# Decoding 64-bit MLP weights to float32: two ScalarE passes and one VectorE pass in place of one and three

## The chip, the cores and the metric

The kernel runs on one core of a Trainium2 chip. The metric is the device time of one launch in microseconds (us), the median of three runs. The core's engines are named as in the profile: PE is TensorE (PEld its weight loads), DVE is VectorE, ACT is ScalarE, POOL is GpSimd, SP is SyncE, which here only starts DMAs. Each engine executes its instructions strictly in the order of the program, and waits for others by semaphores.

## The reference

```python
scores = scale * q @ k.T - log(448)            # 4 batches x 12 heads, 448 x 448, head size 64
x = sigmoid(scores) @ v                        # -> (4, 448, 768)
h = relu(x @ w_in)                             # 768 -> 1024
u, v = h[..., :512], h[..., 512:]
v_n = (v - mean(v)) / sqrt(var(v) + 1e-6)
x = (u * (w_spatial @ v_n + b_spatial)) @ w_out    # 512 -> 768
xn = (x - mean(x)) / sqrt(var(x) + 1e-6) * g_ln
out = x + relu(xn @ w_ch1) @ w_ch2             # 768 -> 3072 -> 768
```

The weights w_in, w_out, w_ch1 and w_ch2 arrive as 64-bit floating-point numbers, which the kernel reads as pairs of 32-bit words, the low word first. It turns them into float32 on the chip. A 64-bit number has an 11-bit exponent and 52 bits of fraction: the high word holds the sign, the exponent and the upper 20 bits of the fraction, and float32 wants 3 more fraction bits, which are the top 3 of the low word.

## The kernel before

**Stages.** The attention runs first, heads in pairs, and hands its result batch by batch to the gated block (w_in, the spatial product, w_out). This stage lasts until about 370 us. Then comes the MLP with w_ch1 and w_ch2, in 24 steps of one weight group each: steps i = 0 to 11 (the loop at L1505) for eight row blocks of the output, the later ones over the same twelve groups for the other six. A group is 256 of the 3072 hidden columns and consists of four chunks of 128 x 768 weights (k = 0, 1 from w_ch1, k = 2, 3 from w_ch2).

**Products.** Nearly every float32 product is three matmuls of split operands (mm3, L317): both factors are split into a high part that PE takes at once (a cast on ACT) and the rest (a subtraction on DVE or POOL). The products with w_ch1 follow a scheme with seven block products in place of eight; B11, B21, T1, T2, B22, T3 and T4 are blocks of the weights or differences of such blocks, and A11, A12, S1, S2, S4, S3 and A22 the same of the activations. Two accumulators are involved in a step: X (a PSUM tile "ps1") and Y ("psa"). Y receives S1 x T1, is copied out by ACT (`copied`, L1258 to L1261, the copy at L1260), and then S4 x B22 is added to it in PSUM. So PE may begin S4 x B22 only after the copy. `summed` (L1263) adds such a copy to another accumulator on DVE (L1264), applies ReLU on ACT (L1266) and takes the low part on DVE (L1269). `ch2` multiplies the hidden block by w_ch2, eight row blocks one after another, and DVE adds each result to the output in SBUF (L911, the "chunk add").

**Decoding a chunk.** `w_scale` (L332 to L339) has ACT multiply the high word, read as a float, by 2^-112, which makes the exponent right and loses the low bits (L338, an ACTIVATE). `bit_ops` (L341 to L354) then makes three DVE passes: shift left by 3 (L345), OR in the low word shifted right by 29 (L347), OR in the sign of the high word (L351). In the attention stage, for groups 0, 1 and 3, `in_place` (L823) does the same inside the raw tile: the low word's shift (L827) and the scale (L828), then two DVE passes (L830, L833). Twelve chunks go this way; the other nine groups, 36 chunks, use `scale` and `bit` during the steps 0 to 11. The tile "q_all" or "m_all" holds raw words, "f_all" floats, "r_all" split parts.

**What sets the order.** The order is written out by hand. `plan1` (L1347) says for each spot of an MLP step which jobs are issued there: `s1` is `scale(1)`, `b1` is the next DVE pass of chunk 1, `T1` a split, `=T1` a difference, `w0` a split of a w_ch2 chunk. A `+` means the next group. In a usual step, spot A1 (right after X has been copied the first time) holds `+b0 +b0 +s1`, so the scale of chunk 1 stands on ACT ahead of the ReLU of `summed` and of the copy of Y. The third `b` of a chunk also issues the load of a later chunk into the raw tile (`load(k + 2)`, or for k = 2, 3 the next group's chunk). In the attention stage a stream (L998) takes jobs such as `i0` from a list, at a rate by assumed costs, and puts them between the attention's own instructions. `i0 i1` ahead of each other make a burst of two scale passes on ACT.

Of the kernel before, what the change touches and what calls it, by code (L numbers as in the profile page):

```python
# [9 lines left out]

F32 = mybir.dt.float32
F32R = mybir.dt.float32r
U32 = mybir.dt.uint32
AF = mybir.ActivationFunctionType
ALU = mybir.AluOpType

P = 128
# [20 lines left out]
WC = 768  # L38
# [116 lines left out]
class Block:  # L155
# [13 lines left out]
    def ap(self, *dims):  # L169
        a = self.bits(*dims)  # L170
        return a.bitcast(F32) if self.t.dtype == U32 else a

# [12 lines left out]
class Ring:  # L185
# [4 lines left out]
    def next(self):  # L190
        self.i += 1
        return self.blocks[(self.i - 1) % len(self.blocks)]
# [66 lines left out]
def sigmoid_attention_gmlp_mlp(ctx: ExitStack, tc, q, k, v, w_in, w_sp, w_out, g_ln, w1, w2, out):  # L259
    nc = tc.nc  # L260
    const = ctx.enter_context(tc.tile_pool(name="const", bufs=1))
# [5 lines left out]

    R = Arena("r", const.tile([P, R_SIZE], F32R, name="r_all"))
    plain = ctx.enter_context(tc.tile_pool(name="plain", bufs=1, side="right"))
    F = Arena("f", plain.tile([P, F_SIZE], U32, name="f_all"))  # L270
    raws = tc.tile_pool(name="raws", bufs=1, side="right")
    Q = Arena("q", raws.__enter__().tile([P, Q_SIZE], U32, name="q_all"))
    mid = tc.tile_pool(name="mid", bufs=1)
    M = Arena("m", mid.__enter__().tile([P, T_SIZE], U32, name="m_all"))
    vscr = dram.tile([NT, DH], F32, name="vscr")
# [18 lines left out]
    vstat = const.tile([P, B, 4, 2], F32, name="vstat")  # L294
    nc.vector.memset(vstat, 1.0)
    vnorm = const.tile([P, 2, B, 4], F32, name="vnorm")
    mhalf = const.tile([P, 2, 4], F32, name="mhalf")
    nc.vector.memset(mhalf, -0.5)

# [27 lines left out]
    def w_load(src, blk=None):  # L327
        raw = (blk or raw_r.next()).bits(WC, 2)
        nc.sync.dma_start(raw.rearrange("p n t -> p (n t)"), src.bitcast(U32))
        return raw  # L330

    def w_scale(raw, pool, blk=None):  # L332
        blk = blk or dec_r.next()
        f, high = blk.ap(WC), raw[:, :, 1].bitcast(F32)
        if pool:
            nc.gpsimd.tensor_scalar(f, high, 2.0**-112, None, op0=ALU.mult)
        else:
            nc.scalar.mul(f, high, 2.0**-112)  # L338
        return blk  # L339

    def bit_ops(raw, blk):  # L341
        bits = blk.bits(WC)
        low, high = raw[:, :, 0], raw[:, :, 1]

        nc.vector.tensor_scalar(bits, bits, 3, None, op0=ALU.logical_shift_left)  # L345
        yield
        nc.vector.scalar_tensor_tensor(  # L347
            bits, low, 29, bits, op0=ALU.logical_shift_right, op1=ALU.bitwise_or
        )
        yield  # L350
        nc.vector.scalar_tensor_tensor(  # L351
            bits, high, 0x80000000, bits, op0=ALU.bitwise_and, op1=ALU.bitwise_or
        )
        yield  # L354
# [10 lines left out]
    class Chunk:  # L365
# [8 lines left out]
        def scale(self, pool=True):  # L374
            self.blk = w_scale(self.raw, pool)
# [234 lines left out]
    def vn_make(b, vf, vn):  # L610


        vh, vl, t1, t2 = (t.ap(t.n // DH, DH) for t in vn)
        t1, t2 = t1[:, 0], t2[:, 0]
        nc.gpsimd.memset(t2[D:P].bitcast(F32), 1.0)
        for c in range(4):
            m = rows(c)
            scale, bias = (vnorm[:m, i, b, c : c + 1] for i in range(2))
            if c in VN_DVE[b]:
                nc.vector.tensor_scalar(vf[:m, c], vf[:m, c], scale, bias, op0=ALU.mult, op1=ALU.add)  # L620
            else:
                nc.scalar.activation(vf[:m, c], vf[:m, c], AF.Identity, scale=scale, bias=bias)
            hi, lo = (vh[:, c], vl[:, c]) if c < 3 else (t1[:D], t1[D:P])
            nc.scalar.copy(hi, vf[:m, c])
            if c:
                nc.vector.tensor_sub(*late)
            late = (lo, vf[:m, c], hi)
            yield
        nc.vector.tensor_sub(*late)
        nc.scalar.copy(t2[:D], t1[:D])  # L630
# [124 lines left out]
    class Group:  # L755
# [10 lines left out]
            self.raw[k] = w_load(src, blk)  # L766

        def scale(self, k):
            w_scale(self.raw[k], False, self.dec[k])
            self.ops[k] = bit_ops(self.raw[k], self.dec[k])  # L770

        def bit(self, k):

            next(self.ops[k])
            self.left[k] -= 1
            if not self.left[k]:
                if k > 1:
                    put(wfscr[self.g, k - 2], self.dec[k].ap(WC))
                if k < 2:
                    self.load(k + 2)  # L780
                elif self.late:
                    self.late.load(k - 2)
# [40 lines left out]
        def in_place(self, k):  # L823

            low, high = (self.raw[k][:, :, i] for i in range(2))
            f = high.bitcast(F32)
            nc.vector.tensor_scalar(low, low, 29, None, op0=ALU.logical_shift_right)  # L827
            nc.scalar.mul(f, f, 2.0**-112)  # L828
            yield
            nc.vector.scalar_tensor_tensor(low, high, 3, low, op0=ALU.logical_shift_left, op1=ALU.bitwise_or)  # L830
            yield
            out = low if k < 2 else self.dec[k - 2].bits(WC)
            nc.vector.scalar_tensor_tensor(out, high, 0x80000000, low, op0=ALU.bitwise_and, op1=ALU.bitwise_or)  # L833
            self.held[k] = out.bitcast(F32)
            yield

# [129 lines left out]
    def put(dst, src):  # L966
        puts.append([5 if now[0] < 10**6 else 2, lambda: nc.sync.dma_start(dst, src.bitcast(F32))])
# [130 lines left out]
    mid.__exit__(None, None, None)  # L1098
    T = Arena("t", ctx.enter_context(tc.tile_pool(name="top", bufs=1, reuse_waits="tile")).tile([P, T_SIZE], F32R, name="t_all"))
    vraw_r = Ring(F, 4 * DH, 1)  # L1100
# [112 lines left out]
    for j, (u, c) in enumerate(order):  # L1213
        u0, n = UNITS[u]
# [38 lines left out]
    def product(ps, x, w, first):  # L1253
        (xh, xl), (wh, wl) = x, w
        for kc in range(HK):
            mm3(ps, wh[:, kc], wl[:, kc], xh[:, kc], xl[:, kc], first and kc == 0, kc == HK - 1, True)

    def copied(x):  # L1258
        t = tmp_r.next().ap(n)
        nc.scalar.copy(t, x)  # L1260
        return t  # L1261

    def summed(u, f, t, y):  # L1263
        nc.vector.tensor_add(t, t, y)  # L1264
        hh, hl = hid[u]
        nc.scalar.activation(hh[f], t, AF.Relu)  # L1266

        def low():
            nc.vector.scalar_tensor_tensor(hl[f], t, 0.0, hh[f], op0=ALU.max, op1=ALU.subtract)  # L1269

        return low
# [11 lines left out]
    n = 4 * P  # L1283
# [221 lines left out]
    for i in range(NGRP):  # L1505
# [32 lines left out]
        t = copied(X)  # L1538
# [4 lines left out]
        low = summed(0, 0, t, Z)  # L1543
# [9 lines left out]
        t = copied(X)  # L1553
# [7 lines left out]
        low = summed(0, 1, t, Y)  # L1561
# [7 lines left out]
        low = summed(1, 1, p5, X)  # L1569
# [20 lines left out]
    n = 3 * P  # L1590
# [10 lines left out]
    t = copied(X)  # L1601
    x_jobs[10]()
    raws.__exit__(None, None, None)
    top_q = tc.tile_pool(name="top_q", bufs=1, side="right", reuse_waits="tile")
    arenas["q"] = Arena("q", ctx.enter_context(top_q).tile([P, Q_SIZE], F32R, name="q2_all"))
    product(Y, xt["S1"], grp.of1("T1"), True)
# [30 lines left out]
    for i in range(NGRP + 1, 2 * NGRP):  # L1637
# [15 lines left out]
        t = copied(X)  # L1653
# [24 lines left out]
        t = copied(X)  # L1678
# [90 lines left out]
```

## Time and profile before

| | |
|---|---|
| device time, median of 3 runs | 1009.86 us (1009.8 to 1010.14) |
| span of the profiled execution | 1005.8 us |
| time that lies around the span | 4.06 us, the difference to the median (the profile gives no other total of this execution) |
| PE busy | 998.7 us, 99% |
| DVE busy | 763.8 us, 76% |
| ACT busy | 428.2 us, 43% |
| POOL busy | 322.2 us, 32% |
| granted PE clock | 1.0 of full speed in all 40 slices |

Busy time is an engine's own instructions, without waits. The chain of waits follows the work that ended last back from the last instruction: 96% of the span is PE, 1% each ACT, DVE and DMA. A group of the table by line gives busy time, mean duration of one, and the idle time ahead of it with what ended it. A timeline row gives start, duration, engine, line, operation and tiles; in brackets stands how long the engine had been idle before and what released it. Matmuls overlap, so their starts tell more than their ends; a PE that waits does so in the weight load ahead of a matmul.

### The profile page before, as it was taken

Reading aid. Unit: us, or ns where it says so; the run is one execution under the profiler, and the core shown is the slowest. Engines: PE = TensorE matmul, PEld = TensorE weight load, DVE = VectorE, ACT = ScalarE, POOL = GpSimd, SP = SyncE. Lnnn points to the kernel's source line nnn. Section 1 sums busy time; section 2 is a strip of 40 time slices with the busy share of each in tenths; the row PEclk is TensorE's granted clock in tenths of the full one; section 3 lists DMA queues with packets and bytes.
Section 4 is the critical chain, followed back from the end, with each engine's and each line's share of the span. In section 5 each row is a group of like instructions: output and inputs, shape, how many; then the busy total and the mean of one; then the engine's idle time right before and its main releaser. Section 6 shows DMA issues by size and latency. Waiting matters only on the chain.

```text
span 1005.8 us, 15019 instructions
## 1 busy us (share of the span) xinstructions
PE 998.7 (99%) x5497; PEld 877.3 (87%) x5497; DVE 763.8 (76%) x1095; ACT 428.2 (43%) x708; POOL 322.2 (32%) x286
## 2 busy tenths in 40 slices
PE   9999999999999999999999999999999999999998
PEld 5566667668999989899998999899999999999998
DVE  3769897627755877767788888876778888988885
ACT  6765555445635742312433334342343334333331
POOL 4532234201213830000533355333043434433330
PEclk9999999999999999999999999999999999999999
DMA  8775989835411367684576878777997677766652
GB/s 240 228 246 200 331 302 333 300 152 166 157 69 48 137 242 269 225 319 173 166 266 233 292 254 274 266 242 247 316 348 231 209 219 225 215 205 209 223 165 94
DMA packets 88649, 227.22 MB, mean 226 GB/s; under 512 B 11520, under 2 KB 39680, under 8 KB 88448
## 3 DMA queue, kind: packets, MB, share of 16 engines
q1 hardware_dynamic: 82688, 210.49, 62.4%
q0 software_dynamic: 2240, 9.72, 2.9%
q10 hardware_dynamic: 3648, 6.06, 1.7%
q8 instruction: 43, 0.70, 0.3%
q14 instruction: 30, 0.25, 0.1%
HBM read 147.31 MB, written 78.92 MB: 225 GB/s over the span
## 4 chain that ended last, share of the span: by engine, by line
PE 96%; ACT 1%; DVE 1%; DMA 1%; issue 0%; ACTq 0%; DVEq 0%
PE ps L318 23%; PE ps L320 23%; PE ps L319 22%; PE psa L512 6%; PE psa L318 5%; PE psa L320 5%; PE psa L319 5%; PE ps L472 5%; PE ps L485 1%; PE psa L499 1%; DMA out_y<-f_all 1%; PE ps L709 1%; ACT f_all L459 0%; PE psa L709 0%; DMA f_all<-in_q 0%; DVE f_all L911 0%
## 5 line engine op out<-in xcount | busy, mean ns | idle before, releaser
L320 PE MATMUL ps<-r_all,t_all 128*128 128x384 f32 (+1 forms) x599 | 205.0, 342 | 0.0
L319 PE MATMUL ps<-r_all,t_all 128*128 128x384 f32 (+1 forms) x599 | 204.9, 342 | 0.0
L318 PE MATMUL ps<-r_all,t_all 128*128 128x384 f32 (+1 forms) x599 | 204.9, 342 | 0.0
L318 PE MATMUL ps<-r_all 128*128 128x384 f32 (+2 forms) x480 | 174.8, 364 | 0.0
L320 PE MATMUL ps<-r_all 128*128 128x384 f32 (+2 forms) x480 | 173.4, 361 | 0.1
L319 PE MATMUL ps<-r_all 128*128 128x384 f32 (+2 forms) x480 | 172.9, 360 | 0.0
L911 DVE TENSOR_TENSOR f_all<-ps,f_all 128x768 f32<-128x768 f32 x96 | 91.7, 955 | 38.6 <-PE ps L320 38.2
L318 PEld LDWEIGHTS ps<-r_all,t_all 128*128 128x128 f32 x599 | 112.6, 188 | 3.1
L319 PEld LDWEIGHTS ps<-r_all,t_all 128*128 128x128 f32 x599 | 112.6, 188 | 3.1
L320 PEld LDWEIGHTS ps<-r_all,t_all 128*128 128x128 f32 x599 | 112.6, 188 | 2.5
L318 PEld LDWEIGHTS ps<-r_all 128*128 128x128 f32 x480 | 90.1, 188 | 11.1 <-issue 3.8
L320 PEld LDWEIGHTS ps<-r_all 128*128 128x128 f32 x480 | 90.1, 188 | 8.9 <-DVE r_all L1442 0.4
L319 PEld LDWEIGHTS ps<-r_all 128*128 128x128 f32 x480 | 90.1, 188 | 7.4
L811 POOL TENSOR_TENSOR r_all<-f_all,r_all 128x384 fp32r<-128x384 f32 x31 | 39.5, 1285 | 173.1 <-DVE t_all L1269 117.9
L459 ACT ACTIVATE f_all<-ps,bias_s 128x896 f32<-128x896 f32 x70 | 68.1, 1005 | 28.6 <-PE ps L485 14.9
L1473 DVE TENSOR_TENSOR f_all<-ps,f_all 128x768 f32<-128x768 f32 x77 | 73.3, 952 | 6.2 <-PE ps L320 4.9
L1427 POOL TENSOR_TENSOR f_all<-f_all 128x384 f32<-128x384 f32 x44 | 49.7, 1130 | 65.1 <-DMA f_all<-wfscr 55.6
L472 PEld LDWEIGHTS ps<-r_all 64*128 64x128 f32 x432 | 37.5, 184 | 28.6 <-issue 16.2
L455 POOL TENSOR_TENSOR r_all<-f_all,r_all 128x384 fp32r<-128x384 f32 x22 | 23.7, 1078 | 112.9 <-DVE r_all L451 109.0
L318 PE MATMUL psa<-r_all 128*128 128x512 f32 (+2 forms) x153 | 57.1, 373 | 0.0
L320 PE MATMUL psa<-r_all 128*128 128x512 f32 (+2 forms) x153 | 56.9, 372 | 0.0
L319 PE MATMUL psa<-r_all 128*128 128x512 f32 (+2 forms) x153 | 56.9, 372 | 0.0
(241 smaller groups left out, 1956.2 us busy)
## 6 DMA issues: line engine op xcount, KB each, us to landing
q_all<-in_w SPq DMA_DIRECT2D x42, 768.0 KB, 5.9
r_all<-w1scr SPq DMA_DIRECT2D x65, 384.0 KB, 3.6
w1scr<-r_all SPq DMA_DIRECT2D x61, 384.0 KB, 4.9
w2scr<-r_all SPq DMA_DIRECT2D x24, 768.0 KB, 7.8
t_all<-w1scr SPq DMA_DIRECT2D x40, 384.0 KB, 3.7
r_all<-w2scr SPq DMA_DIRECT2D x37, 384.0 KB, 4.3
wfscr<-f_all SPq DMA_DIRECT2D x24, 384.0 KB, 6.5
w1scr<-t_all SPq DMA_DIRECT2D x23, 384.0 KB, 5.5
```

Of the source, the lines that this page charges most:

```text
L318: nc.tensor.matmul(ps, lh, rh, start=first, stop=False, skip_group_check=skip)
L319: nc.tensor.matmul(ps, lh, rl, start=False, stop=False, skip_group_check=skip)
L320: nc.tensor.matmul(ps, ll, rh, start=False, stop=last, skip_group_check=skip)
L455: eng.tensor_sub(kl, kr[:, :SM], kh)
L459: nc.scalar.activation(af, ps[:, :, :S], AF.Sigmoid, bias=bias_s, scale=1.0 / math.sqrt(D))
L472: nc.tensor.matmul(ps[:, j, :S], a[w][rows, kc], a[x][rows], start=(i == 0), stop=(i == 2))
L485: nc.tensor.matmul(ps[D * i : D * i + D, j, :S], kr[rows, SM:S], qr[rows], start=True, stop=True)
L512: nc.tensor.matmul(a["ps"][rows, :S], a["v"][:, 4 * j + c], af[:, j], start=(p % 2 == 0 and c == 0), stop=(p % 2 == 1 and c == 2),)
L811: eng.tensor_sub(t[:, 1], x, t[:, 0])
L911: nc.vector.tensor_add(y[:, hs], ps, y[:, hs])
L1427: nc.gpsimd.tensor_sub(self.f(*out), self.f(*a), self.f(*b))
L1473: nc.vector.tensor_add(y[:, :2, u, s], two, y[:, :2, u, s])
```

## The change

For the 48 chunks of w_ch1 and w_ch2, the scale pass on ACT becomes a parametric ReLU (`signed`): for positive values the factor is 2^-112, for negative values additionally 2^32, which raises the exponent by 32 and so sets the bit that a shift left by 3 moves into the sign's place. A second ACT pass (`low_bits`) reads the upper 16 bits of the low word as an unsigned integer, multiplies by 2^-13, adds a constant from a small tile (`bias_d`) and writes the integer result, the three bits wanted, over the low word. One DVE pass (`bits_of`) shifts the first result left by 3 and ORs in the second. The job strings are as before: of three `b` jobs of a chunk the first two now issue nothing, and the third issues the DVE pass and then the same stores and loads as before. In `in_place` both ACT passes come with the first job, and the DVE pass with the third. The w_in and w_out chunks keep the old passes. Lines after the change are higher by 17 or 18: L1260 is now L1277, L1266 is L1283, L911 is L928.

```diff
--- before.py
+++ after.py
@@ -10,6 +10,7 @@
 
 F32 = mybir.dt.float32
 F32R = mybir.dt.float32r
+U16 = mybir.dt.uint16
 U32 = mybir.dt.uint32
 AF = mybir.ActivationFunctionType
 ALU = mybir.AluOpType
@@ -294,6 +295,8 @@
     vstat = const.tile([P, B, 4, 2], F32, name="vstat")
     nc.vector.memset(vstat, 1.0)
     vnorm = const.tile([P, 2, B, 4], F32, name="vnorm")
+    bias_d = const.tile([P, 1], F32, name="bias_d")
+    nc.vector.memset(bias_d, 2.0**-14 - 0.5)
     mhalf = const.tile([P, 2, 4], F32, name="mhalf")
     nc.vector.memset(mhalf, -0.5)
 
@@ -337,6 +340,21 @@
         else:
             nc.scalar.mul(f, high, 2.0**-112)
         return blk
+
+    def signed(f, high):
+
+        nc.scalar.activation(f, high, AF.Prelu, scale=2.0**-112, alpha=2.0**32)
+
+    def low_bits(raw):
+
+        top = raw.rearrange("p n t -> p (n t)").bitcast(U16).rearrange("p (n t) -> p n t", t=4)[:, :, 1]
+        nc.scalar.activation(raw[:, :, 0], top, AF.Identity, bias=bias_d, scale=2.0**-13)
+
+    def bits_of(out, f, raw):
+
+        nc.vector.scalar_tensor_tensor(
+            out, f, 3, raw[:, :, 0], op0=ALU.logical_shift_left, op1=ALU.bitwise_or
+        )
 
     def bit_ops(raw, blk):
         bits = blk.bits(WC)
@@ -766,14 +784,15 @@
             self.raw[k] = w_load(src, blk)
 
         def scale(self, k):
-            w_scale(self.raw[k], False, self.dec[k])
-            self.ops[k] = bit_ops(self.raw[k], self.dec[k])
+            raw = self.raw[k]
+            signed(self.dec[k].ap(WC), raw[:, :, 1].bitcast(F32))
+            low_bits(raw)
 
         def bit(self, k):
 
-            next(self.ops[k])
             self.left[k] -= 1
             if not self.left[k]:
+                bits_of(self.dec[k].bits(WC), self.dec[k].bits(WC), self.raw[k])
                 if k > 1:
                     put(wfscr[self.g, k - 2], self.dec[k].ap(WC))
                 if k < 2:
@@ -823,14 +842,12 @@
         def in_place(self, k):
 
             low, high = (self.raw[k][:, :, i] for i in range(2))
-            f = high.bitcast(F32)
-            nc.vector.tensor_scalar(low, low, 29, None, op0=ALU.logical_shift_right)
-            nc.scalar.mul(f, f, 2.0**-112)
+            signed(high.bitcast(F32), high.bitcast(F32))
+            low_bits(self.raw[k])
             yield
-            nc.vector.scalar_tensor_tensor(low, high, 3, low, op0=ALU.logical_shift_left, op1=ALU.bitwise_or)
             yield
             out = low if k < 2 else self.dec[k - 2].bits(WC)
-            nc.vector.scalar_tensor_tensor(out, high, 0x80000000, low, op0=ALU.bitwise_and, op1=ALU.bitwise_or)
+            bits_of(out, high, self.raw[k])
             self.held[k] = out.bitcast(F32)
             yield
```

On ACT, in the attention stage at the burst near 141 us, before the change (L459 is the sigmoid, L362 the cast of a split; q_all is the raw tile):

```order
L459 ACTIVATE m_all<-ps_1291,bias_s 128x896
L362 CAST r_all<-psa 128x448
L828 ACTIVATE q_all<-q_all 128x768 x2
L459 ACTIVATE f_all<-ps_1322,bias_s 128x896
L459 ACTIVATE f_all<-ps_1330,bias_s 128x896
```

and after it, the same place:

```order
L477 ACTIVATE m_all<-ps_1287,bias_s 128x896
L380 CAST r_all<-psa 128x448
L346 ACTIVATE q_all<-q_all 128x768
L351 ACTIVATE q_all<-q_all,bias_d 128x768
L346 ACTIVATE q_all<-q_all 128x768
L351 ACTIVATE q_all<-q_all,bias_d 128x768
L477 ACTIVATE f_all<-ps_1318,bias_s 128x896
L477 ACTIVATE f_all<-ps_1326,bias_s 128x896
```

Two more passes (L351 of the changed kernel) stand between the cast and the sigmoid. On ACT in a usual MLP step, from the cast of a w_ch2 chunk (L845) to the copy of Y (the L1260 that reads psa), before:

```order
L845 CAST r_all<-f_all 128x768
L926 ACTIVATE t_all<-ps_4582 128x512
L338 ACTIVATE f_all<-q_all 128x768
L1260 COPY f_all<-ps_4827 128x512
L338 ACTIVATE f_all<-q_all 128x768
L1266 ACTIVATE t_all<-f_all 128x512
L1260 COPY f_all<-psa 128x512
```

and after:

```order
L862 CAST r_all<-f_all 128x768
L943 ACTIVATE t_all<-ps_4556 128x512
L346 ACTIVATE f_all<-q_all 128x768
L351 ACTIVATE q_all<-q_all,bias_d 128x768
L1277 COPY f_all<-ps_4797 128x512
L346 ACTIVATE f_all<-q_all 128x768
L351 ACTIVATE q_all<-q_all,bias_d 128x768
L1283 ACTIVATE t_all<-f_all 128x512
L1277 COPY f_all<-psa 128x512
```

A second pass follows each scale, the one of chunk 1 ahead of the ReLU and of the copy of Y. On DVE, from the low half of a ReLU (L1269) over four chunk adds (L911) to the third pass of a chunk (L351, which is followed by the load of another chunk), before:

```order
L1269 SCALAR_TENSOR_TENSOR t_all<-f_all,t_all 128x512
L911 TENSOR_TENSOR f_all<-ps_5010,f_all 128x768
L345 TENSOR_SCALAR f_all<-f_all 128x768
L911 TENSOR_TENSOR f_all<-ps_5026,f_all 128x768
L347 SCALAR_TENSOR_TENSOR f_all<-q_all,f_all 128x768
L911 TENSOR_TENSOR f_all<-ps_5041,f_all 128x768
L351 SCALAR_TENSOR_TENSOR f_all<-q_all,f_all 128x768
L846 TENSOR_TENSOR r_all<-f_all,r_all 128x768
```

and after:

```order
L1286 SCALAR_TENSOR_TENSOR t_all<-f_all,t_all 128x512
L928 TENSOR_TENSOR f_all<-ps_4978,f_all 128x768
L928 TENSOR_TENSOR f_all<-ps_4993,f_all 128x768
L928 TENSOR_TENSOR f_all<-ps_5007,f_all 128x768
L355 SCALAR_TENSOR_TENSOR f_all<-f_all,q_all 128x768
L863 TENSOR_TENSOR r_all<-f_all,r_all 128x768
```

Between the adds the two passes are gone; the last one is where it was. PE and POOL have the same instructions in the same order in both kernels, and so has SP its DMAs.

## Rows read from the trace of the kernel before

**Rows 1.** The page's first part: busy us, share of the span, instructions.

```profile
PE 998.7 (99%) x5497; PEld 877.3 (87%) x5497; DVE 763.8 (76%) x1095; ACT 428.2 (43%) x708; POOL 322.2 (32%) x286
```

**Rows 2.** The chain of waits, 141 to 145 us: start, duration, engine, tile, line.

```profile
141.47 1.67 ACT q_all L828 x2
143.13 0.89 ACT f_all L459
144.06 0.97 PE psa L512 x4
```

**Rows 3.** Waits of PE's weight loads: total us, times, longest us.

```profile
PEld psa L512 <- issue: 25.8, 105, 0.7
PEld ps L472 <- issue: 16.2, 23, 0.7
...
PEld psa L512 <- DVE r_all L363: 2.5, 8, 0.3
```

**Rows 4.** Groups by line and shape: busy us, mean ns | idle before, releaser.

```profile
L338 ACT ACTIVATE f_all<-q_all 128x768 f32<-128x768 f32 x40 | 36.1, 902 | 32.2 <-DMA q_all<-in_w 32.2
...
L345 DVE TENSOR_SCALAR f_all<-f_all 128x768 uint32<-128x768 uint32 x48 | 31.7, 661 | 14.3 <-ACT f_all L338 13.6
...
L347 DVE SCALAR_TENSOR_TENSOR f_all<-q_all,f_all 128x768 uint32<-128x768 uint32 x44 | 45.9, 1044 | 0.8
...
L362 ACT CAST r_all<-f_all 128x1152 fp32r<-128x1152 f32 x4 | 4.6, 1151 | 8.8 <-DVE f_all L1302 8.8
```

**Rows 5.** Timeline of MLP step i = 7: start, duration, engine [idle before, releaser].

```profile
569.17 0.96 DVE L911 TENSOR_TENSOR f_all<-ps,f_all 128x768 f32<-128x768 f32 x1 [0.26 <-PE ps L320]
570.04 0.95 DVE L351 SCALAR_TENSOR_TENSOR f_all<-q_all,f_all 128x768 uint32<-128x768 uint32 x1
...
571.05 0.33 SPq L329 DMA_DIRECT2D q_all<-in_w  x1
...
577.02 0.89 ACT L338 ACTIVATE f_all<-q_all 128x768 f32<-128x768 f32 x1 [3.15 <-DMA q_all<-in_w]
...
578.33 0.57 ACT L1260 COPY f_all<-psa 128x512 f32<-128x512 f32 x1
...
578.98 0.19 PEld L318 LDWEIGHTS psa<-r_all,t_all 128*128 128x128 f32 x1
...
579.44 0.39 PE L319 MATMUL psa<-r_all,t_all 128*128 128x512 f32 x1
```

**Rows 6.** Timeline of ACT at 347 us.

```profile
347.62 0.94 ACT L702 ACTIVATE f_all<-f_all,rs 128x768 f32<-128x768 f32 x1
348.46 0.47 ACT L730 CAST r_all<-psa 128x384 fp32r<-128x384 f32 x1
348.82 0.49 ACT L731 COPY f_all<-psa 128x384 f32<-128x384 f32 x1
```

**Rows 7.** Timeline of ACT and PE at 116 us.

```profile
116.09 0.99 ACT L459 ACTIVATE f_all<-ps,bias_s 128x896 f32<-128x896 f32 x1
...
116.31 1.70 PE L472 MATMUL ps<-r_all 64*128 64x448 f32 x12
```

**Rows 8.** Timeline of DVE and PE at 84 to 87 us.

```profile
84.25 1.78 DVE L363 TENSOR_TENSOR r_all<-f_all,r_all 128x768 fp32r<-128x768 f32 x1
...
86.90 0.37 PE L320 MATMUL ps<-r_all 128*128 128x448 f32 x1
```

**Rows 9.** Timeline of the copy of Y in step i = 5.

```profile
515.81 0.57 ACT L1260 COPY f_all<-psa 128x512 f32<-128x512 f32 x1
...
516.72 0.19 PEld L318 LDWEIGHTS psa<-r_all,t_all 128*128 128x128 f32 x1
```

**Rows 10.** Timeline of PE after a wait, at 369 us.

```profile
369.09 0.50 PE L318 MATMUL psa<-r_all 128*128 128x512 f32 x1
369.42 0.40 PE L319 MATMUL psa<-r_all 128*128 128x512 f32 x1
```

**Rows 11.** Timeline of ACT at the start of the span.

```profile
1.37 1.28 ACT L290 ACT_TABLE_LOAD   x1 [1.37 <-PEq L1759]
```

## The prediction

> **What bounds the kernel now.** I read the engines' busy time first: the tensor engine (PE) is busy for 998.7 of 1005.8 us, VectorE (DVE) for 763.8 and ScalarE (ACT) for 428.2 [rows 1]. PE is the bound, so an ACT or DVE pass counts only where PE ends up waiting for it. The chain of waits says the same: it is PE nearly all the way, and it leaves PE for an ACT row on a decode burst at one place only, at 141 us, where two decode passes stand between a split and the sigmoid that PE's attention product needs [rows 2]. Then I read what PE's weight loads waited for: of DVE, 2.5 us for the low halves of the attention (L363) [rows 3], the largest such wait by far and so most of what a less busy DVE could give back directly. Last I went through the timeline at each place where a decode stands on ACT, and looked for the next PE instruction that needs something issued behind it on ACT.
>
> **What the change removes.** Each of the 48 chunks of MLP weights loses two of its three DVE passes. In the 36 chunks of the MLP stage these are L345 and L347, 0.661 and 1.044 us [rows 4]: 36 x 1.705 = 61 us. In the 12 chunks decoded inside the attention their counterparts L827 and L830 go, at the same durations another 20. So DVE loses some 80 of its 764 us. I cost this at nothing. What covers it is that the DVE work PE waits for in the MLP is the chunk add L911, and that add waits for PE (0.26 us before the one at 569.17) [rows 5], not for DVE's queue. The third pass stays where it was, directly behind the fourth chunk add, and with it the weight load of the next chunk.
>
> **What it adds.** One ACT pass of 128x768 per chunk, 48 in all, each issued straight behind the pass that was there. No row has this operation (a 16-bit source, four elements apart, with a bias pointer). The nearest is L338, 902 ns, which reads every second word of the same tile [rows 4]; by start to start, which is what counts in a queue, a 768-column pass with a pointer operand moves the next one by 348.46 - 347.62 = 0.84 us, and two passes of L828 before the next start take 1.67, so 0.83 each [rows 2, 6]. I take 0.845. From below the bound is a pass at half the columns, 348.82 - 348.46 = 0.36 us [rows 6], should a 16-bit source go twice as fast; from above it is the longest ACT pass of the trace, 1152 columns at 1.15 us with no overlap [rows 4]. I take the middle value because the row nearest in shape has it.
>
> The Trainium skill, "ScalarE: Activation LUTs", Rules for kernel authors, says that multiplies and adds belong on VectorE, not on ScalarE, since DVE is faster per element. The trace agrees for this tile, 661 ns for L345 on DVE against 902 for L338 on ACT. If the pass cost 0.66 where I put 0.845, the sum below would be near 1014.5; and by that rule the change hands work to the slower of two engines, neither of which is the bound.
>
> **Where ACT's pass is on the path: the attention.** Twelve chunks come in bursts of two, so a burst gets longer by 2 x 0.845 = 1.69 us.
> At 141.47 the burst is on the chain: split, two L828 passes, sigmoid L459 at 143.13, then PE's L512 at 144.06 [rows 2]. PE has nothing else to do, so +1.69.
> At 114.45 the sigmoid at 116.09 waits behind the burst and releases the second half of the score block L472, a block of 12 that took 1.70 us with that wait in it [rows 7]. +1.69.
> At 81.75 the burst stands in front of a cast whose low half L363 at 84.25 (1.78 us, far over the 0.96 of L911 at the same width) feeds the PE product whose last part starts at 86.90 [rows 8]. Moved 1.69 later, to 85.94, and without that stretch, L363 would end at about 86.9: +0.15, between 0 and 1. The other bursts (102, 150 to 153, 175 us) end over an ACT pass's length ahead of what PE needs next, or wait for their DMA in any case; I cost them at nothing.
>
> **Where it is on the path: the MLP stage.** Per group of weights, ACT does this: L338 on chunk 1, which waits for the DMA (until 577.02 in the group shown), L1266, then the copy of Y out of PSUM, L1260, at 578.33 to 578.90. PE's next product into Y may start only after the copy; its weight load is at 578.98, so 0.08 us of slack [rows 5]. The DMA was issued at 571.05, right behind L911 and L351, which themselves follow PE [rows 5]; it moves with PE, not with DVE. The new pass stands between L338 and L1266, so the copy comes 0.845 later. Six groups have this shape (i = 5 to 10). From copy end to weight load they have 0.34 (copy at 515.81 for 0.57, weight load at 516.72), 0.25, 0.08, 0.24, 0.15 and 0.43 us [rows 5, 9], which are two of the six, together 1.49, less some 0.05 each from release to load: 1.19 usable. A late weight load also gives a little back, since the second matmul follows the first by 0.33 us after a wait (369.09 to 369.42) [rows 10] where 0.46 lies between weight load and second matmul undisturbed (578.98 to 579.44) [rows 5]: 0.13 each, 0.78 in all. So 6 x 0.845 - 1.19 - 0.78 = 3.1 us. The groups i = 1 to 4 and 11 have over 1.2 us between that copy and PE, and cost nothing.
>
> **The sum.** 1.69 + 1.69 + 0.15 + 3.1 = 6.6 us on PE; with one more bias constant set at the start, 6.7. All is worked from an execution whose span is 1005.8 us; the median of the runs is 1009.86, so 4.06 us lie around the span, and nothing of the change is there. 1009.86 + 6.7 = **1016.5 us**. With the pass at 0.36 it would be 4 x 0.36 = 1.4, and 0.4 more from the groups with little slack: 1011.7. With 1.15 it would be 4.6 + 0.85 (81.75 is then fully late) + 6.9 - 1.97 = 10.4: 1020.3.
>
> **The rivals.**
> *The MLP waits are absorbed.* If the chunk's load lands at least 0.7 us earlier in the six groups, the new pass runs in that time and only the attention remains: 1009.86 + 3.5 = 1013.4. For it: DVE has one pass less between its adds. Against it: the pass ahead of the load's issue, L351, starts right after an add that waited for PE [rows 5].
> *The new pass is slower*, 1.0 to 1.15 us: 10 x 1.0 - 1.8 = 8.2, and 10.4 as above, so 1018.1 to 1020.3, 1019.5 as its value. For it: 16-bit reads at an 8-byte step and an in-place write are not in the trace. Against it: L338 and L828 also step by two words, and cost what a plain pass costs.
> *Not slower: DVE's relief comes through on PE.* The place is the attention, where PE's weight loads waited 2.5 us for DVE, and 25.8 + 16.2 us for nothing that the trace names, in waits of 0.25 us in L512 (25.8 over 105) [rows 3]. If the first vanishes and a tenth of the second (4.2 us) was DVE's doing, 6.7 us come back: 1009.86 + 6.7 - 6.7 = 1009.9. It decides from 4.7 us of relief on. Against it: the nameless waits are alike all through the attention, while only six short bursts of it have decodes.
> *Not slower: a short pass*, 0.35 us or less: 1.4 + 0.4 us, so 1011.6. Against it: no 768-column row of ACT is under 0.8.
> *A table reload.* If parametric ReLU needed another function table than the sigmoid, each burst and each chunk would carry loads like the one at the start, 1.28 us [rows 11]: two more at each of the two attention bursts and each of the six groups, 16 x 1.28 = 20 us, so about 1037. ACT's instructions in order have one table load, as before, so this is next to excluded.
> The Trainium skill, "ScalarE: Activation LUTs", Table sets: the hidden batching unit, says that tables come as sets and that a function outside the loaded set costs a load and a drain; the 1.28 us row is its load, and no row here shows what set this function is in.
>
> **How the numbers follow.** Forecast 0.66 (its own range 1014.5 to 1018), absorbed 0.10, slower pass 0.11, DVE's relief 0.07, short pass 0.04, table reload 0.02. A difference under 0.2%, about 2 us, can't be told from none. Faster is a relief of over 8.7 us, half of the relief case, 0.04 with rounding; within 0.2% are the other half and the short pass, 0.07; slower is the rest, 0.89. The range goes from 1012.5, under the absorbed case and at a pass of 0.45 us, to 1020.3, the upper bound of the pass; outside are the short pass, the relief, the reload and some of the tails, under 0.2.
>
> **What would show it.** Right: DVE's busy time down by some 80 us and ACT's up by about 40; the new pass at 0.8 to 0.95 us; the chain through two more ACT rows per burst at about 114 and 141 us; PE weight loads that wait 0.4 to 0.7 us for L1277 (the copy) in six groups; as many adds that wait for PE as before. Wrong: if PE shows no wait on that copy (absorbed), if the pass lasts over 1 us, if the unnamed PE waits shrink by microseconds, or if a second table load stands in the trace.

## The result and the profile after

The changed kernel takes 1021.17 us (median; 1018.29 to 1021.47) against 1009.83 for the kernel before: ratio 1.0107, 95% interval 1.0091 to 1.0122. That is +11.3 us between the medians and +10.8 by the ratio. The forecast was slower by 6.7 us. The direction held, the time lies 0.9 us above the range.

The changed kernel's page begins with the engines' busy time:

```profile
PE 1005.1 (99%) x5497; PEld 881.1 (86%) x5497; DVE 689.2 (68%) x1000; ACT 468.9 (46%) x756; POOL 313.3 (31%) x286
```

DVE lost 75 us and ACT gained 41 [rows 1], near the forecast 80 and 40. The chunk add before the change, and the chunk add and the new pass after it, in the tables by line and shape:

```profile
L911 DVE TENSOR_TENSOR f_all<-ps,f_all 128x768 f32<-128x768 f32 x96 | 91.7, 955 | 38.6 <-PE ps L320 38.2
```

```profile
L928 DVE TENSOR_TENSOR f_all<-ps,f_all 128x768 f32<-128x768 f32 x96 | 91.7, 956 | 74.0 <-PE ps L323 73.8
...
L351 ACT ACTIVATE q_all<-q_all,bias_d 128x768 uint32<-128x768 uint16 x42 | 41.4, 985 | 0.0
```

The pass lasts 985 ns. The relieved DVE waits for PE before these adds for 73.8 us, where it waited 38.2: half of the 75 us stands there as idle time. In the chain of waits, the burst at 141 us now reads:

```profile
144.78 0.88 ACT q_all L351
145.67 0.81 ACT q_all L346
146.48 0.90 ACT q_all L351
147.38 0.89 ACT f_all L477
148.27 0.04 issue
148.31 0.97 PE psa L530 x4
```

Two L351 rows of 0.9 us stand where [rows 2] had none, and in the matmuls' starts, laid beside those of before, PE falls 1.74 us further behind here. At 117 us it is 1.71 us. Step i = 7, in the timeline:

```profile
583.85 0.90 ACT L346 ACTIVATE f_all<-q_all 128x768 f32<-128x768 f32 x1 [3.05 <-DMA q_all<-in_w]
584.64 0.96 ACT L351 ACTIVATE q_all<-q_all,bias_d 128x768 uint32<-128x768 uint16 x1
585.51 0.62 ACT L1283 ACTIVATE t_all<-f_all 128x512 fp32r<-128x512 f32 x1
586.03 0.56 ACT L1277 COPY f_all<-psa 128x512 f32<-128x512 f32 x1
...
586.64 0.19 PEld L321 LDWEIGHTS psa<-r_all,t_all 128*128 128x128 f32 x1 [0.88 <-ACT f_all L1277]
...
586.98 0.40 PE L322 MATMUL psa<-r_all,t_all 128*128 128x512 f32 x1
```

The pass sits between DMA, ReLU and copy as in the order, costs 0.87 us start to start, and the weight load, which waited for nothing in [rows 5], waits 0.88 us. The waits of PE's weight loads (total us, times, longest):

```profile
PEld psa L530 <- issue: 25.5, 104, 0.7
...
PEld psa L321 <- ACT f_all L1277: 4.6, 6, 0.9
...
PEld psa L530 <- ACT f_all L477: 3.5, 3, 2.6
...
PEld ps L321 <- ACT r_all L1455: 2.3, 1, 2.3
```

Six waits for the copy are there, and the waits without a name are as before [rows 3]. The last row was not foreseen. It stands at the change of halves, where the ReLU of the first result of the second half writes into a block whose output store must have landed. The chain of waits there:

```profile
747.24 6.91 DMA out_y<-f_all
...
754.24 0.54 ACT f_all L1463
...
754.79 0.52 ACT r_all L1455
...
755.34 3.31 DVE r_all L1459 x2
758.65 0.47 DVE f_all L1644
...
759.15 0.53 ACT f_all L1463
...
759.71 0.52 ACT r_all L1455
...
760.27 0.44 PE ps L321
```

In the kernel before the same places, in the chain of waits, in the timelines of ACT and DVE and among the waits of PE's weight loads, are:

```profile
737.02 5.72 DMA out_y<-f_all
...
742.82 0.53 ACT L1446 ACTIVATE f_all<-f_all 128x384 f32<-128x384 f32 x1 [1.80 <-DMA out_y<-f_all]
...
743.93 0.90 DVE L1442 TENSOR_TENSOR r_all<-f_all,r_all 128x384 fp32r<-128x384 f32 x1
...
745.32 0.80 DVE L1442 TENSOR_TENSOR r_all<-f_all,r_all 128x384 fp32r<-128x384 f32 x1 [0.48 <-ACT r_all L1438]
...
747.17 0.52 ACT L1438 CAST r_all<-f_all 128x384 fp32r<-128x384 f32 x1
...
PEld ps L320 <- DVE r_all L1442: 0.4, 1, 0.4
```

There too ACT waited for the store, and the cast at 747.17 ended 0.07 us before PE's matmul at 747.76, which needs it: no slack. The matmul two further on even waited 0.4 us for the low half. In the changed kernel the store came some 1.1 us later against PE's progress, and the two DVE passes, now begun beside a POOL subtraction that had started first, took 2.02 and 1.37 us in place of 0.90 and 0.80. The Trainium skill, "SBUF — State Buffer", SBUF: two separate sides, says that a DVE operation with two SBUF inputs and a GpSimd operation that reads SBUF share a port pair, which the first to start holds to its end. The trace agrees that a pass begun behind POOL's is held: the first of the two, which lasts 0.56 us alone, ended 0.4 us after the second of two POOL passes. The windows behind it (busy us of PE, PEld, DVE, ACT, POOL, then the granted clock):

```profile
750.00:760.00 10.00, 8.27 (x48) 7.95 (x46) 5.17 (x6) 4.52 (x10) 7.81 (x9) 1.00 1.01 372
762.00:764.00 2.00, 2.00 (x8) 2.00 (x8) 1.24 (x3) 1.00 (x3) 0.00 (x0) 0.50 0.94 373
```

After a wait of 2.3 us the matmuls run at half clock (0.50, the 1.2 GHz level) for some 3 us, at 0.32 us each in place of 0.18: another 1.5 us. Laying the two traces side by side, the changed kernel's 14.2 us on PE are: start of the attention 0.7, burst at 81 us 0.2, bursts at 117 and 144 us 3.45, six copies 3.6, change of halves 3.8 with its half clock, and 2.4 us that come from no wait at all: matmuls between 380 and 745 us simply start further apart. The start differs from execution to execution, and the profile of before had the earliest of all that were taken (the others lose 0.5 to 2.9 us in the first 20). The two spans lie 13.8 apart and the medians 11.3. So the 4.06 us that the prediction puts around the span are in part this early start: in the changed kernel's profiled execution, 1021.47 us with a span of 1019.6, only 1.9 us lie there. This changes nothing in the forecast, which adds the sum to the median.

### The profile page after: what moved, and what is told of

The parts are those of the page before. It is cut to its first block, busy times and chain, and to the rows that moved or that the text cites. A ratio compares the mean times of both kernels' runs of the same rounds, so it can differ in the third digit from the quotient of the medians.

```text
span 1019.6 us, 14947 instructions
## 1 busy us (share of the span) xinstructions
PE 1005.1 (99%) x5497; PEld 881.1 (86%) x5497; DVE 689.2 (68%) x1000; ACT 468.9 (46%) x756; POOL 313.3 (31%) x286
## 4 chain that ended last, share of the span: by engine, by line
PE 89%; DMA 5%; ACT 3%; DVE 2%; issue 1%; ACTq 0%; DVEq 0%
PE ps L321 21%; PE ps L323 21%; PE ps L322 21%; PE psa L530 6%; PE ps L490 5%; PE psa L321 4%; PE psa L323 4%; PE psa L322 4%; DMA q_all<-in_w 3%; PE ps L503 1%; PE psa L517 1%; ACT q_all L351 1%; DMA out_y<-f_all 1%; DVE f_all L355 1%; ACT f_all L346 1%
## 5 line engine op out<-in xcount | busy, mean ns | idle before, releaser
L323 PE MATMUL ps<-r_all 128*128 128x384 f32 (+2 forms) x480 | 173.7, 362 | 0.0
L928 DVE TENSOR_TENSOR f_all<-ps,f_all 128x768 f32<-128x768 f32 x96 | 91.7, 956 | 74.0 <-PE ps L323 73.8
L830 POOL TENSOR_TENSOR r_all<-f_all,r_all 128x384 fp32r<-128x384 f32 x31 | 35.6, 1159 | 179.5 <-ACT r_all L829 163.1
L473 POOL TENSOR_TENSOR r_all<-f_all,r_all 128x384 fp32r<-128x384 f32 x22 | 23.7, 1077 | 117.7 <-DVE r_all L469 113.1
```

The lines of the kernel that those rows point to most:

```text
L323: nc.tensor.matmul(ps, ll, rh, start=False, stop=last, skip_group_check=skip)
L473: eng.tensor_sub(kl, kr[:, :SM], kh)
L830: eng.tensor_sub(t[:, 1], x, t[:, 0])
L928: nc.vector.tensor_add(y[:, hs], ps, y[:, hs])
```

## The experiments

Every kernel is timed against the kernel before on the same chip, in five rounds. Kernels that stand under ctl to signed_only share a chip, and so do those under after_again to late, under att_noshift to ctl_pad3, and the last four; the four chips differ. A gain or loss in us is worked out from the ratio.

**ctl.** Only the change's constant, unused, added to the kernel before:

```diff
+    bias_d = const.tile([P, 1], F32, name="bias_d")
+    nc.vector.memset(bias_d, 2.0**-14 - 0.5)
     mhalf = const.tile([P, 2, 4], F32, name="mhalf")
```

> The kernel before with the one constant of the change (bias_d) set at the start and not used. Both theories: 1009.8 us, no change. It is here to see how far a second profiled execution of the same work lies from the one shown (span 1005.8), at the start (first scores at 5.46 us before, 6.12 after the change), in the matmul spacing of the MLP stage, and at the change of halves near 748 us, where the changed kernel lost 2.2 us to a wait and 1.5 more at the half clock. If that loss is an accident of the chip, some runs of this kernel show a granted clock under 1 too.

Measured: 1012.1, ratio 1.0013 (1.0002 to 1.0024). Between 380 and 740 us its trace has no new wait, and yet PE falls 2.2 us behind the trace of before. Only matmuls that read t_all are affected. At 748 us it loses nothing.

**att_only and mlp_only.** The changed kernel with the old code put back in `scale` and `bit` (att_only) or in `in_place` (mlp_only).

The edit of att_only begins:

```diff
-            raw = self.raw[k]
-            signed(self.dec[k].ap(WC), raw[:, :, 1].bitcast(F32))
-            low_bits(raw)
+            w_scale(self.raw[k], False, self.dec[k])
+            self.ops[k] = bit_ops(self.raw[k], self.dec[k])
...
```

> Two ACT passes and one DVE pass only for the 12 chunks decoded in the attention; the 36 chunks of the MLP stage as before. Theory A (the second ACT pass costs where PE waits for ACT, here two bursts of two passes): +3.6 us, so 1013.4, with the two steps near 117 and 144 us of 1.7 us each. Theory B (any shift of PE against the DMA queues also brings the loss at the change of halves near 748 us): +7, so 1017, with a granted clock under 1.

> Two ACT passes and one DVE pass only for the 36 chunks of the MLP stage; the 12 chunks of the attention as before. Theory A: +3.6 us in six steps of 0.6 (a weight load waits for the copy of Y), so 1013.4, and no loss near 748 us if that was an accident. Theory B (the passes in the MLP stage bring the loss at the change of halves): +7.3, so 1017, with a granted clock under 1.

Measured: 1.0064 (1.0046 to 1.0083) and 1.0056 (1.0037 to 1.0076), so +6.5 and +5.7: both over theory A, and the intervals reach up to B's +7 and +7.3, so the times alone don't exclude B. The traces do: they have the steps of A (1.68 and 1.74; six, of 0.6 on average), at 748 us only 0.3 and 0.2, and both have the 2.2 us of ctl.

**signed_only.** The parametric ReLU kept, the low word's shift back on DVE at the second job:

```diff
...
-        nc.scalar.activation(raw[:, :, 0], top, AF.Identity, bias=bias_d, scale=2.0**-13)
+        low = raw[:, :, 0]
+        nc.vector.tensor_scalar(low, low, 29, None, op0=ALU.logical_shift_right)
...
+            if self.left[k] == 1:
+                low_bits(self.raw[k])
```

> All 48 chunks with the parametric ReLU as the one ACT pass, the low word's shift as a DVE pass, and one DVE pass to put both together: ACT as before the change in number and place, DVE with two passes in place of three. Theory A (relief of DVE is worth nothing to PE, the cost lies in the second ACT pass alone): 1009.8, within 1 us. Rival (DVE's relief counts, and was only hidden by ACT's cost): 1007 or less. Rival (the parametric ReLU itself is dear): over 1012.

Measured: 1.0009 (0.9997 to 1.0021), as ctl. A third of the bit work taken off DVE is worth nothing that can be measured, and the parametric ReLU costs nothing.

That four different programs shared one unexplained loss led to theory C. Constants take 32 bytes each in a partition, by the addresses in the built programs; the new one moves t_all, the tile of the hidden activations, from byte 144096 to 144128. The attention's tile m_all, which lies in the same place, and some small tiles move too; r_all, f_all and q_all stay.

**after_again, after_noshift, ctl_pad.** The changed kernel once more; the same with the constant in a second column of the sigmoid's bias tile; and the kernel before with two constants, so 64 bytes.

```diff
-    bias_s = const.tile([P, 1], F32, name="bias_s")
+    bias = const.tile([P, 2], F32, name="bias")
+    bias_s, bias_d = bias[:, 0:1], bias[:, 1:2]
...
-    bias_d = const.tile([P, 1], F32, name="bias_d")
```

> The changed kernel unaltered, for a second profiled execution and for its time on the chip of this comparison. Theory A+C (two bursts of two passes in the attention 3.4 us, six copies in the MLP stage 3.6, and 2.5 for matmuls that read t_all, which the new constant's 32-byte slot moves from byte 144096 of a partition to 144128): +9.5 us where the wait at the change of halves near 748 us stays away, up to +13 where it comes. Rival (that wait, 2.2 us and 1.5 at the half clock, belongs to the change and comes in every run): +13 with a granted clock under 1 in every run.

> The changed kernel with its constant in a second column of the tile that holds the sigmoid's bias, so that no tile moves (t_all at byte 144096 as in the kernel before). Theory C (the tile's place costs): median spacing of the w_ch2 matmuls back at 173 to 174 ns from 175 to 176, 2.5 us less than the changed kernel. Rival D (the spacing is that of the chip or the execution): as the changed kernel.

> The kernel before with two unused constants, which move t_all by 64 bytes to 144160. Theory C with the place counted in 64 bytes: as the kernel before, 0 to 0.3 us, spacing 173 to 174 ns. With the place counted in 128 bytes: as with one constant, +1.3 to +2.5. Rival D: as with one constant.

Measured: after_again 1.0107 (1.0092 to 1.0122), after_noshift 1.0075 (1.0057 to 1.0093), ctl_pad 1.0036 (1.0023 to 1.0050). The first repeats the result; its profiled execution has no step at 748 us, but half-clock matmuls behind the wait at 144 us (1.5 us). With the tile back in its place 3.2 us go (about 2.3 either way, by the two intervals). The same two matmuls, 594 apart and with no wait between them, in the timelines of the kernel before, of ctl and of after_noshift:

```profile
383.02 0.39 PE L320 MATMUL ps<-r_all,t_all 128*128 128x512 f32 x1
...
500.16 0.34 PE L320 MATMUL ps<-r_all,t_all 128*128 128x384 f32 x1
```

```profile
386.13 0.40 PE L322 MATMUL ps<-r_all,t_all 128*128 128x512 f32 x1
...
504.07 0.34 PE L322 MATMUL ps<-r_all,t_all 128*128 128x384 f32 x1
```

```profile
391.22 0.39 PE L323 MATMUL ps<-r_all,t_all 128*128 128x512 f32 x1
...
508.38 0.34 PE L323 MATMUL ps<-r_all,t_all 128*128 128x384 f32 x1
```

117.14, 117.94 and 117.16 us: the stretch costs 0.8 us more with the tile moved, and nothing more with all passes changed but the tile in place. So rival D falls. ctl_pad, on the chip of after_noshift, has 118.32, so 64 bytes are worse than 32, which neither form of C had. In after_noshift half-clock matmuls follow both attention waits. Its windows around the first:

```profile
117.00:120.70 3.70, 2.12 (x22) 0.79 (x14) 0.00 (x0) 3.70 (x6) 0.00 (x0) 1.00 0.95 349
...
122.40:125.00 2.60, 2.60 (x10) 0.88 (x8) 0.00 (x0) 0.52 (x1) 0.00 (x0) 0.55 0.95 357
```

PE was busy for 2.12 of 3.70 us, and from about 122 us the clock is near half, which costs 1.6 us on top of the 1.68 of the wait itself.

**late.** after_noshift, with the second ACT pass issued by a chunk's second job, and in a usual step one job moved behind the copy of Y:

```diff
             self.left[k] -= 1
+            if self.left[k] == 1:
+                low_bits(self.raw[k])
...
-            A1="+b0 +b0 +s1", A2="+b1 +b1", A3="+b1 +B11 +B21" + ("" if i - 1 in AHEAD else " w1"),
+            A1="+b0 +b0 +s1", A2="+b1", A3="+b1 +b1 +B11 +B21" + ("" if i - 1 in AHEAD else " w1"),
```

> The constant in the sigmoid's tile again, and the second ACT pass issued later: with a chunk's second job in place of its first, and for chunk 1 of a usual MLP step behind the copy of Y (one job moved from spot A2 to A3). Number of passes on ACT and DVE as in the changed kernel. Theory A: the six waits for the copy go, 3.6 us less than with the constant's place alone mended; in the attention the burst at 141 us loses its two passes in front of the sigmoid (1.7 less), and the one at 114 keeps up to 1.7. In all +0.5 to +3 over the kernel before. Rival (ACT's total work is what counts): as the kernel with the constant's place mended, +7.

Measured: 1.0001 (0.9989 to 1.0012), so +0.1, under theory A's +0.5 to +3. The same passes on the same engines, and the whole cost is gone, that of the burst at 114 us too. Step i = 7 in its timeline:

```profile
580.03 0.56 ACT L1278 COPY f_all<-psa 128x512 f32<-128x512 f32 x1
580.49 0.98 ACT L351 ACTIVATE q_all<-q_all,bias 128x768 uint32<-128x768 uint16 x1
...
580.64 0.19 PEld L321 LDWEIGHTS psa<-r_all,t_all 128*128 128x128 f32 x1 [0.17 <-ACT f_all L1278]
```

The copy comes first, the pass of 0.98 us behind it, and the weight load follows the copy by 0.05.

**att_noshift and mlp_noshift.** att_only and mlp_only with the constant in the sigmoid's tile, by the edit of after_noshift.

> The new passes for the 12 chunks of the attention alone, with the constant in the sigmoid's tile, so that no tile moves; the MLP stage decodes as before. Theory A: 3.4 us in two waits of 1.7 us more (117 and 144 us), and some half-clock matmuls behind those waits in some runs, so +3.4 to +5. Rival (the attention costs more than its two waits show): over +5.5, which is what the run with the moved tile had.

> The new passes for the 36 chunks of the MLP stage alone, with the constant in the sigmoid's tile; the attention decodes as before. Theory A: 3.5 us in six waits for the copy of Y, nothing else: +3.5, and together with the run for the attention alone as much as the changed kernel without the moved tile (+7.6). Rival (the stages' costs don't add up, since a wait in one lets transfers catch up in the other): +2 or less, or +5 or more.

Measured: 1.0042 (1.0026 to 1.0059) and 1.0033 (1.0019 to 1.0048), so +4.2 and +3.4, together 7.6, as much as after_noshift's. The attention is its two waits, 3.4 us, and half-clock matmuls in part of the executions (1.5 us at 144 us in the profiled one). mlp_noshift's profiled execution has the step at 748 us (2.2 us), so that step needs no passes in the attention. It doesn't need the new passes at all: signed_only, which has no second ACT pass, loses 1.1 us there, and ctl_pad3 (below), the kernel before with nothing but constants added, loses 1.2. In ctl_pad3's timeline and among its waits:

```profile
742.86 0.53 ACT L1450 ACTIVATE f_all<-f_all 128x384 f32<-128x384 f32 x1 [3.01 <-DMA out_y<-f_all]
...
PEld ps L322 <- ACT r_all L1442: 1.4, 1, 1.4
```

**pool.** The kernel before with the attention's scale on GpSimd:

```diff
-            nc.scalar.mul(f, f, 2.0**-112)
+            nc.gpsimd.tensor_scalar(f, f, 2.0**-112, None, op0=ALU.mult)
```

> The kernel before, with the scale pass of the 12 chunks of the attention on GpSimd in place of ScalarE, so that no decode stands in front of a sigmoid; everything else as before. Theory A: PE's waits of the kernel before for the sigmoid behind a decode go (0.9 us at 144 us and 0.3 near 117): -1.2 us, so that it beats both kernels by 0.1%. Rival: the pass takes 2.2 us on GpSimd, as the strided scale of the first chunks does, and holds up DVE's passes, on which the low halves for PE wait (2.5 us of waits before): +1 or more.

Measured: 1.0100 (1.0082 to 1.0117), +10, against theory A. The waits for the sigmoid shrink a little (0.3 us at 144), but at 163 us PE waits 8.7 us. Its timeline there:

```profile
164.68 0.82 POOL L589 DMA_DIRECT2D vstat<-sscr  x1 [9.31 <-DMA sscr<-vraws]
...
167.39 4.39 POOL L828 TENSOR_SCALAR m_all<-m_all 128x768 f32<-128x768 f32 x2
...
172.82 0.29 PEld L512 LDWEIGHTS psa<-m_all 128*64 128x64 f32 x4 [8.71 <-DVE r_all L363]
```

The scale was queued on POOL behind a DMA issue that waited 9.31 us for another transfer, DVE's pass behind the scale, and PE's low half behind that. The rival named the right chain and half of the reason: the two passes do take 2.2 us each there (4.39), but they could begin only at 167.39, behind the DMA issues.

**ctl_pad3.** The kernel before with 96 bytes of unused constants, t_all at 144192:

```diff
+    bias_d = const.tile([P, 1], F32, name="bias_d")
+    nc.vector.memset(bias_d, 2.0**-14 - 0.5)
+    pad = const.tile([P, 16], F32, name="pad")
+    nc.vector.memset(pad, 0.0)
```

> The kernel before with 96 bytes of unused constants, which move t_all to byte 144192. Where 32 bytes cost 1.8 ns for each of some 1340 matmuls and 64 bytes 2.4, a place counted in 128 bytes or a distance that only grows both give 2 ns or more, +2.5 us or more; a place counted in 64 bytes was excluded by the run with 64. Rival: this place is as good as the one before, 0 to 0.3 us.

Measured: 0.9973 (0.9961 to 0.9984), faster than the kernel before, which neither side expected. The two matmuls:

```profile
383.50 0.39 PE L324 MATMUL ps<-r_all,t_all 128*128 128x512 f32 x1
...
500.08 0.34 PE L324 MATMUL ps<-r_all,t_all 128*128 128x384 f32 x1
```

116.58 us. So by place of t_all: 117.14 at 144096, 117.94 at 144128, 118.32 at 144160, 116.58 at 144192. The profiled executions of all the kernels here agree with it, on whatever chip: 117.1 to 117.2 us in the six with the tile at 144096, 117.9 to 118.0 in the seven at 144128, and 116.6 in the four at 144192.

**after_pad3, after_edge, late_pad3, late_pad3_edge.** The changed kernel with t_all at 144192; the changed kernel with `r_r.i = 2` behind the ring's creation, so that the first ReLUs of the second half take blocks whose stores are long done; late with 96 bytes more; and late with both.

> The changed kernel with 64 bytes of unused constant beside its own, so that t_all lies at byte 144192, where the kernel before with 96 bytes gained 0.27%. Theory C (the place of t_all is a cost by itself, apart from the passes): the changed kernel's +10.8 less 2.5 and less another 2 to 2.7, so +5.5 to +6.5 over the kernel before. Rival (the gain at 144192 was another effect of that run): +8, as with the tile in its first place.

> The changed kernel with the ring of MLP result blocks at the change of halves started two blocks further, so that the first ReLU there no longer waits for the last output store. Theory E (the wait near 748 us, 2.2 us and 1.5 at the half clock in the first profiled execution, is that store landing late in front of a chain without slack): no step near 748 us, and a median 0.5 to 2 us under the changed kernel's. Rival (the chain there waits for something else, or for POOL beside DVE): the step is there as before, and the time is the same.

> The second ACT pass issued late, as in the run that was level with the kernel before, and t_all at byte 144192. If both effects add up: 0.25% faster than the kernel before, 1007.5, faster than both kernels. If the late passes only seemed free because a run was lucky: slower than the kernel before.

> As the run with late passes and t_all at 144192, with the ring of result blocks started two blocks further. Theory E: another 0.3 to 1 us less, 1007. Rival: the same, or more where a later use of a block waits instead.

Measured: after_pad3 1.0040 (1.0023 to 1.0058), better than forecast: the place is a cost by itself. after_edge 1.0082 (1.0062 to 1.0102) against 1.0107: some 2.5 us less, but the two were timed on different chips and the intervals overlap, so that the store costs time on average is not shown. In its trace the ReLU waits only for the sum, and PE's step at 748 us is 0.2 us:

```profile
752.43 0.53 ACT L1463 ACTIVATE f_all<-f_all 128x384 f32<-128x384 f32 x1 [1.35 <-DVE f_all L1633]
```

late_pad3 takes 1007.3 us, 0.9966 (0.9952 to 0.9979), and late_pad3_edge 1007.0, 0.9965 (0.9952 to 0.9977): both faster than both kernels, by the tile's place alone. The other ring start adds nothing measurable there, against theory E's 0.3 to 1 us, although the profiled execution of late_pad3 has a step of 1.2 us at 748.

## Why the prediction was wrong

The mechanism was right where it was worked out. One term of the sum, the new constant, was put at next to nothing and is the step that failed; two others were a little small. Timed with the tile of the hidden activations in its place, the attention costs 4.2 us and the MLP stage 3.4, together the 7.6 of after_noshift; with the 3.2 for the tile's place that makes the changed kernel's 10.8.

- **What bounds, and DVE's relief at nothing: right.** Of the 75 us off DVE, half shows as longer waits for PE before the chunk adds; signed_only is level with ctl, and late, with all of the relief, is level with the kernel before.
- **The pass at 0.845 us: a little small.** Each pass added made a burst 0.86 to 0.87 us longer (from start to start 0.89 to 0.90, while the pass ahead of it went from 0.83 to 0.81), and in the MLP it is 0.87 start to start, though one pass by itself lasts 985 ns, over the 0.8 to 0.95 of the prediction's signs.
- **The attention, 1.69 twice and 0.15: right, but not whole.** The steps are 1.71, 1.74 and 0.19. Left out was what PE does after such a wait: with about 2.6 us of waiting at 144 us, the matmuls behind it ran at half clock in four of the seven profiled kernels that have these passes (after_again, after_noshift, att_noshift, after_pad3), for 1.5 us. Timed, the attention is 4.2.
- **The six copies, 3.1: a little small.** They cost 3.6 in the trace and 3.4 timed (mlp_noshift). The weight loads waited 0.5 to 0.9 us, 4.6 in all, where 0.4 to 0.7 was forecast: the pass is longer, and less of the slack of 1.19 could be used. The credit of 0.13 for the matmul after a late weight load held: from weight load to second matmul it is 0.34 us (586.64 to 586.98) in place of 0.46.
- **"With one more bias constant set at the start, 6.7": failed.** This is the largest error. The prediction priced the memset, at 0.1 us, which no row of before shows, and not the address. The constant moves t_all by 32 bytes, and the 384-column matmuls of steps 0 to 11 that read it start some 2 ns further apart: 2.2 us in the trace of ctl, 1.3 timed, 3.2 timed in the changed kernel (after_noshift against after_again).
- **The change of halves: not in the sum, and open.** The trace of before had the signs: its chain of waits runs through the output store, and PE waited 0.4 us behind it. The place cost 3.8 us in the first profiled execution of the changed kernel and nothing in the second. Why the store lands late in some executions stays open, and so does whether the change makes it likelier: mlp_noshift has the step, att_noshift hardly, and signed_only and ctl_pad3 have it in part without the second pass. The sum of the timed runs above needs no term for it.
- **The rivals.** None of them happened. What the forecast lacked is no slower pass (0.87 to 0.90 us from start to start, where that rival has 1.0 to 1.15) and no table reload (one table load stands in the trace, as before). It is the tile's place for the most part, then the half clock and the copies.

## What to carry to other kernels

An added pass costs what stands behind it in its queue: here the same 48 passes cost 7.6 us in front of a sigmoid and a copy, and nothing one job later. A new constant is also an address: put it where no large tile moves, or compare with a run that has only the constant. When looking for slack, follow the chain through the engines and transfers that feed the bound too: one that ends 0.07 us before it is needed shows no wait there yet.

## What the runs showed of the hardware

- The spacing of 384-column fp32r matmuls depends on where the stationary operand's tile begins. Over the 1144 pairs of such matmuls on t_all that stand one straight behind the other (between 375 and 745 us of the kernel before), the mean from start to start is 173.7, 176.0, 176.6 and 173.3 ns for t_all at bytes 144096 (before), 144128 (ctl), 144160 (ctl_pad) and 144192 (ctl_pad3) of a partition, the moving operand unmoved. What rule lies behind these four places was not tried.
- Half clock after single waits: 0.50 to 0.55 of full speed (the 1.2 GHz level) for some 3 us behind weight loads that had waited 2.0 to 2.6 us in some executions, and full clock behind the same wait in others.
- An ACT pass from 16-bit words eight bytes apart to 32-bit words in place, with a bias pointer, takes 985 ns for 768 columns, 82 more than the 32-bit pass without one beside it (903): the smaller source showed no gain.
